# Loading all of k ahead of q and giving the first weight products banks of their own, in a cross-covariance attention and SwiGLU kernel

## The chip, the cores and the metric

The kernel runs on one core of a Trainium2 chip. The metric is the time of one execution on the device in microseconds (us), the median of several; the profile's span of the same execution is about 2 us shorter, because it runs from the first instruction to the last. The engines are called PE (matrix products), PEld (its weight loads), ACT (ScalarE), DVE (VectorE), POOL (GpSimd, which issues the casting loads here) and SP.

## The reference

Four batches of 6016 rows by 256 channels go through attention across channels, and the result through a gated feed-forward block:

```python
qn = q / (norm(q, axis=1) + 1e-6)           # q, k, v: (4, 6016, 256)
kn = k / (norm(k, axis=1) + 1e-6)
s = kn.transpose(0, 2, 1) @ qn / tau        # (4, 256, 256), tau = 1
a = softmax(s, axis=-1)
x = (v @ a).reshape(24064, 256)
g = x @ w_gate                              # (24064, 1536)
out = (silu(g) * (x @ w_val)) @ w_out       # (24064, 256)
```

## The kernel before

The kernel folds the attention matrix into the weights: per batch it forms Wg = a @ w_gate and Wv = a @ w_val, and a main loop then runs v through Wg, Wv and w_out. The work on batch b + 1 (squares, products of k and q, softmax, folding) is spread over the loop of batch b. For batch 0 nothing can hide it, so there is a prologue of some 41 us, and the change is in that prologue and the first steps of the loop only.

PSUM is the memory that PE writes its products to. The kernel lays it out in eight banks and gives each a job: two rotating banks each for the loop's gate and value products (tags "g" and "v"), two rotating ones for outputs (tag "o"), one for the products of k and q ("kq") and one for small sums ("misc"):

```python
psum_gv = tile_pool(name="psum_gv", bufs=2, space=PSUM)   # tags "g" and "v": 4 banks
psum_o  = tile_pool(name="psum_o",  bufs=2, space=PSUM)
psum_kq = tile_pool(name="psum_kq", bufs=1, space=PSUM)
psum_m  = tile_pool(name="psum_m",  bufs=1, space=PSUM)
```

Loads of k and q come in groups of four slabs, k three groups ahead of q. All squares of k are on DVE, those of q (but for the very last pair) on ACT, and PE adds up rows and forms the products as groups arrive:

```python
for g, which in order:                  # k0 k1 k2 k3 q0 k4 q1 ... k11 q8 q9 q10 q11
    if which == 0 and g == NG - 1:
        first_last_q(0, ts)             # the last q group: squares, row copy, products, column sums
        continue
    for t in ts:
        if which == 0:
            gemm1_pair(0, t)
        first_row_sums(0, t, which, first_square(0, t, which, on_dve=(which == 1)), ...)
```

At the end of `first_softmax` the first four folding products ("units" 0 to 3: two of w_gate, two of w_val, 512 columns each) are made in halves, because the loop's first steps need only the lower half. Both halves of a unit share one bank:

```python
for u in range(4):
    wp_evacuate(b, u, units[u], lo)                # ACT for even units, DVE for odd ones
nc.scalar.preload_act_table(ACT.Silu)
for u in range(4):
    for jh in range(CH):
        wp_matmul(b, u, jh, units[u], hi)          # the upper half of the same bank
    wp_evacuate(b, u, units[u], hi, on_dve=True)
```

The loop's step then makes one gate and one value product, a SiLU on ACT and a product on DVE, and in the first chunk two further units after each step:

```python
def gv_step(b, ci, f, sv):
    ...                                            # g_ps and v_ps, two matmuls of 512 columns each
    nc.scalar.activation(silu, g_ps, ACT.Silu)
    nc.vector.tensor_mul(sv[:, f, :], silu, v_ps)

for f in range(FH):                                # 12 steps
    gv_step(b, ci, f, sv)
    if gi == 0:
        for u in range(4 + 2 * f, min(6 + 2 * f, 12)):
            wp_unit(0, u, psum_o, "o")
```

Of the kernel before, what the change touches and what calls it, by code (L numbers as in the profile page):

```python
# [17 lines left out]
def kernel(  # L18
# [11 lines left out]
    nc = tc.nc  # L30
# [145 lines left out]
            nc.tensor.matmul(state[b, "ss", which], ones_bf, sq[:, s, :],  # L176
                             start=(t == 0 and s == 0), stop=(t == t_last and s == pm - 1))

    def first_last_q(b, ts):

        sqs = [first_square(b, t, 0, on_dve=(t == NP - 1)) for t in ts]
        row = work.tile([1, C], FP32, tag="row")
        nc.vector.tensor_copy(row, state[b, "ss", 0][0:1, :])
        for t in ts:
            gemm1_pair(b, t)
        cols = psum_gv.tile([P, CH], FP32, tag="g")
        for h in range(CH):
            nc.tensor.matmul(cols[:, h:h + 1], row[0:1, h * P:(h + 1) * P],
                             ones_f[0:1, 0:1], start=(h == 0), stop=False,
                             skip_group_check=True)  # L190
        for t, sq in zip(ts, sqs):
            pm = pairs[t][1]
            for s in range(pm):
                for h in range(CH):
                    nc.tensor.matmul(cols[:, h:h + 1], sq[:, s, h * P:(h + 1) * P],
                                     ones_bf[:, 0:1], start=False,
                                     stop=(t == ts[-1] and s == pm - 1),
                                     skip_group_check=True)
        state[b, "cols"] = cols

    def first_root(dst, src):
        nc.scalar.activation(dst, src, ACT.Ln)
# [5 lines left out]
        nc.vector.tensor_scalar_add(ink, in0=ink, scalar1=1e-6)  # L208
        state[b, "ink"] = ink

    def first_inv_k(b, h):
        part = state[b, "ink"][:, h * P:(h + 1) * P]
        nc.vector.reciprocal(part, part)

    def first_softmax(b):
        kq, ink = state[b, "kq"], state[b, "ink"]
        inq = work.tile([P, CH], FP32, tag="inq")
        first_root(inq, state[b, "cols"])
        s_f = work.tile([P, CH, C], FP32, tag="s_f")
        nc.vector.tensor_mul(s_f[:, 0, :], kq[:, 0, :], ink)  # L220
        nc.vector.tensor_scalar_add(inq, in0=inq, scalar1=1e-6)
        nc.vector.reciprocal(inq, inq)
        if inv_tau != 1.0:
            nc.vector.tensor_scalar_mul(inq, in0=inq, scalar1=inv_tau)
        nc.vector.tensor_mul(s_f[:, 1, :], kq[:, 1, :], ink)
        transpose_first_v()
        keep_warm(3)
        for h in range(CH):
            evacuate_first_v(h)
        exT = attn.tile([P, CH, C], BF16, tag="exT")  # L230
        state[b, "exT"] = exT
        rs = psum_m.tile([P, CH], FP32, tag="misc")
        for jh in range(CH):
            nc.scalar.activation(exT[:, jh, :], s_f[:, jh, :], ACT.Exp,
                                 scale=inq[:, jh:jh + 1])


        units = []
        for u in range(2 * CH):
            unit_ps = psum_gv.tile([P, WP], FP32, tag="gv"[u % 2])  # L240
            units.append(unit_ps)

        def row_sum(jh):
            for ih in range(CH):
                nc.tensor.matmul(rs[:, ih:ih + 1], exT[:, jh, ih * P:(ih + 1) * P],
                                 ones_bf[:, 0:1], start=(jh == 0 and ih == 0),
                                 stop=(jh == CH - 1), skip_group_check=True)

        HW = WP // 2
        lo, hi = slice(0, HW), slice(HW, WP)  # L250
        row_sum(0)
        wp_matmul(b, 0, 0, units[0], lo)
        wp_matmul(b, 1, 0, units[1], lo)
        row_sum(1)
        finish_rs(b, rs)
        wp_matmul(b, 0, 1, units[0], lo)
        wp_matmul(b, 1, 1, units[1], lo)
        for u in (2, 3):
            for jh in range(CH):
                wp_matmul(b, u, jh, units[u], lo)  # L260
        for u in range(4):
            wp_evacuate(b, u, units[u], lo)
        nc.scalar.preload_act_table(ACT.Silu)
        for u in range(4):
            for jh in range(CH):
                wp_matmul(b, u, jh, units[u], hi)
            wp_evacuate(b, u, units[u], hi, on_dve=True)

    def norm_acc(b, t):
        q_sb, k_sb = qk_tiles[b]  # L270
# [96 lines left out]

    wp_units = [(wc, w, ih) for wc in range(NWC) for w in range(2) for ih in range(CH)]

    def wp_matmul(b, u, jh, ps, part=slice(0, WP)):  # L370
        wc, w, ih = wp_units[u]
        cols = slice(wc * WP + part.start, wc * WP + part.stop)
        nc.tensor.matmul(ps[:, part], state[b, "exT"][:, jh, ih * P:(ih + 1) * P],  # L373
                         (w_gate_sb, w_val_sb)[w][:, jh, cols],
                         start=(jh == 0), stop=(jh == CH - 1), skip_group_check=True)

    def wp_evacuate(b, u, ps, part=slice(0, WP), on_dve=False):
        wc, w, ih = wp_units[u]
        scale = state[b, "smr"][:, ih:ih + 1]
        cols = slice(wc * WP + part.start, wc * WP + part.stop)  # L380
        dst = state[b, "W"][w][:, ih, cols]
        if u % 2 == 0 and not on_dve:
            nc.scalar.activation(dst, ps[:, part], ACT.Copy, scale=scale)
        else:
            nc.vector.tensor_scalar_mul(dst, in0=ps[:, part], scalar1=scale)

    def wp_unit(b, u, pool=psum_m, tag="misc"):

        ps = pool.tile([P, WP], FP32, tag=tag)
        for jh in range(CH):  # L390
            wp_matmul(b, u, jh, ps)
        wp_evacuate(b, u, ps)

    def gv_step(b, ci, f, sv):
        cs, cm = chunks[ci]
# [87 lines left out]


    NG = len(groups)
    K_AHEAD = 3
    order = []
    for g in range(NG + K_AHEAD):
        if g < NG:
            order.append((g, 1))  # L490
        if g >= K_AHEAD:
            order.append((g - K_AHEAD, 0))
    for n, (g, which) in enumerate(order):
        load_qk(0, g, which)
        if n == 8:
# [6 lines left out]
    load_w(1)  # L502
    load_w(2)
    nc.gpsimd.dma_start(out=w_out_sb, in_=moe_w_out.rearrange("(h l) d -> l h d", l=P))
    keep_warm(10)
    T_COLS = groups[NG - 1][0] // 2
    for g, which in order:
        gs, gm = groups[g]
        ts = range(gs // 2, (gs + gm + 1) // 2)
        if which == 0 and g == NG - 1:  # L510
            first_last_q(0, ts)
            continue
        for t in ts:
            if which == 0:
                gemm1_pair(0, t)
            first_row_sums(0, t, which, first_square(0, t, which, on_dve=(which == 1)),
                           (T_COLS if which == 0 else NP) - 1)
        if which == 0:

            after_k = g - (NG - 1 - K_AHEAD)  # L520
            if after_k == 0:
                first_norm_k(0)
                nc.vector.tensor_copy(ident, identf)
            elif 1 <= after_k <= CH:
                first_inv_k(0, after_k - 1)
    first_softmax(0)
    NFIRST = 2 * CH

    prev = None
    for gi, (b, ci) in enumerate(allc):  # L530
        sv = svpool.tile([P, FH, CS * P], BF16, tag="sv")
        for f in range(FH):
            gv_step(b, ci, f, sv)
            if gi == 0:
                for u in range(NFIRST + 2 * f, min(NFIRST + 2 * f + 2, len(wp_units))):
                    wp_unit(0, u, psum_o, "o")
            if prev is not None:
                prev.emit(prev.cm)
            if b + 1 < B:
# [40 lines left out]
```

## Time and profile before

| | |
|---|---|
| time, median of 3 runs | 823.39 us (823.39 to 823.43) |
| span of the profiled run | 821.8 us (that run took 823.9 us) |
| PE busy after 41.07 us | 769.53 of 780.73 us |
| start of the loop's first product | 41.07 us |

This is the start of the loop's third step in the timeline of PE (columns: start, duration, engine, line, operation, output and inputs, shape, count):

```profile
44.52 0.59 PE L404 MATMUL g_ps<-vT_new,Wg 128*128 128x512 bf16 x2
```

By then the kernel before has made units 4 to 7; the changed kernel only 4 and 5.

### The profile page before, as it was taken

The page shows a single profiled execution, that of the slowest core. Times are in us where ns is not written, and L with a number is a line of the kernel's source. Part 1 is how long each engine was busy: PE and PEld are TensorE (multiplying, and loading weights), DVE is VectorE, ACT ScalarE, POOL GpSimd, SP SyncE. Part 2 cuts the span into 40 slices and gives each one's busy share as a digit, 9 for nine tenths or more (in the row PEclk, how much of TensorE's full clock was granted, in tenths as well). Part 3 has the DMA queues.
Part 4 walks back from the last instruction along what each step waited for, and adds up shares of the span by engine and source line. Part 5 has one row for each costly group of instructions (what it writes and reads, how often), then busy time and mean ns, then how long its engine had stood idle before and what let it go on. Part 6 is the DMA issues. An engine that isn't in the chain of part 4 may idle for free.

```text
span 821.8 us, 13520 instructions
## 1 busy us (share of the span) xinstructions
PE 800.2 (97%) x4937; PEld 489.6 (60%) x5024; DVE 552.4 (67%) x870; ACT 461.8 (56%) x826; POOL 90.1 (11%) x171
## 2 busy tenths in 40 slices
PE   7799999999999999999999999999999999999998
PEld 4556566665665566565565656666556565666656
DVE  5576888675655888867556688877665555555554
ACT  2566777555445677645545677755544544544543
POOL 5433000133200000024300000013000000000000
PEclk9999999999999999999999999999999999999999
DMA  9999912169942121129991111125912112112101
GB/s 88 145 160 134 135 39 65 39 119 140 144 90 46 39 65 45 47 52 147 143 150 52 46 52 39 40 65 107 166 39 65 45 40 65 52 39 65 49 26 58
DMA packets 92673, 64.57 MB, mean 79 GB/s; under 512 B 52560, under 2 KB 91472, under 8 KB 91856
## 3 DMA queue, kind: packets, MB, share of 16 engines
q0 software_dynamic: 18656, 27.01, 26.0%
q1 hardware_dynamic: 73952, 36.71, 18.4%
q8 instruction: 39, 0.64, 0.3%
q14 instruction: 26, 0.21, 0.1%
HBM read 78.64 MB, written 36.70 MB: 140 GB/s over the span
## 4 chain that ended last, share of the span: by engine, by line
PE 92%; DMA 3%; ACT 2%; DVE 2%; issue 1%; POOL 0%; DVEq 0%; ACTq 0%; POOLq 0%
PE o_new L432 30%; PE v_ps L404 29%; PE g_ps L404 28%; DMA q_sb<-in_q_dram 2%; PE ps L373 2%; PE kq_new L149 2%; ACT sq L274 1%; DVE sv L408 1%; DMA k_sb<-in_k_dram 1%; DVE acc_new L283 1%; PE cs L291 0%; PE ss_new L176 0%; ACT sq L166 0%; ACT silu L407 0%; PE unit_ps L373 0%
## 5 line engine op out<-in xcount | busy, mean ns | idle before, releaser
L408 DVE TENSOR_TENSOR sv<-silu,v_ps 128x512 bf16<-128x512 bf16 (+1 forms) x576 | 382.6, 673 | 220.1 <-ACT silu L407 218.9
L407 ACT ACTIVATE silu<-g_ps 128x512 bf16<-128x512 f32 (+1 forms) x576 | 337.5, 587 | 305.2 <-PE g_ps L404 252.1
L432 PE MATMUL o_new<-w_out_sb,sv 128*128 128x256 bf16 x2256 | 338.4, 273 | 1.5
L404 PE MATMUL v_ps<-vT,Wv 128*128 128x512 bf16 (+1 forms) x1100 | 324.3, 374 | 6.2 <-DVE sv L408 3.5
L404 PE MATMUL g_ps<-vT,Wg 128*128 128x512 bf16 (+1 forms) x1075 | 319.7, 375 | 0.2
L432 PEld LDWEIGHTS <-sv 128*128 128x128 bf16 x2256 | 220.7, 98 | 140.8
L404 PEld LDWEIGHTS <-Wv 128*128 128x128 bf16 x1152 | 112.7, 98 | 135.0 <-issue 5.4
L404 PEld LDWEIGHTS <-Wg 128*128 128x128 bf16 x1152 | 107.1, 98 | 27.6 <-issue 0.2
L283 DVE TENSOR_TENSOR acc_new<-acc_new,sq 128x512 f32<-128x512 f32 x135 | 93.3, 691 | 23.6 <-ACT sq L274 21.2
L274 ACT ACTIVATE sq<-q_sb 128x512 bf16<-128x512 fp8e5 x72 | 44.3, 615 | 0.0
L274 ACT ACTIVATE sq<-k_sb 128x512 bf16<-128x512 fp8e5 x72 | 44.1, 612 | 0.0
L149 PE MATMUL kq_new<-k_sb,q_sb 128*128 128x512 fp8e5 x184 | 43.3, 317 | 0.3 <-DMA k_sb<-in_k_dram 0.3
L295 POOL TENSOR_TENSOR inv<-inv,half 128x4 f32<-128x4 f32 x3 | 3.1, 1035 | 343.9 <-DVE inv L294 343.9
L441 ACT COPY o_sb<-o_new 128x512 f32<-128x512 f32 x48 | 28.1, 585 | 14.0 <-PE o_new L432 13.7
L443 DVE COPY o_sb<-o_new 128x512 f32<-128x512 f32 (+1 forms) x48 | 31.8, 662 | 3.0 <-PE o_new L432 3.0
L104 POOL DMA_DIRECT2D q_sb<-in_q_dram x48 | 26.1, 544 | 40.1 <-DMA q_sb<-in_q_dram 15.1
L104 POOL DMA_DIRECT2D k_sb<-in_k_dram x48 | 25.9, 540 | 39.5 <-DMA q_sb<-in_q_dram 20.8
L112 POOL DMA_DIRECT2D vb<-in_v_dram x47 | 23.6, 505 | 23.3 <-DMA k_sb<-in_k_dram 14.2
L176 PE MATMUL ss_new<-sq,ones_bf 128*128 128x256 bf16 x91 | 18.3, 285 | 7.5 <-DVE sq L163 6.2
L163 DVE TENSOR_TENSOR sq<-k_sb 128x512 bf16<-128x512 fp8e5 (+1 forms) x24 | 15.2, 681 | 14.2 <-DMA k_sb<-in_k_dram 12.5
L166 ACT ACTIVATE sq<-q_sb 128x512 bf16<-128x512 fp8e5 x23 | 13.0, 619 | 20.1 <-DMA q_sb<-in_q_dram 16.6
L149 PEld LDWEIGHTS <-q_sb 128*128 128x256 fp8e5 x184 | 23.1, 140 | 2.0 <-DMA q_sb<-in_q_dram 0.8
(79 smaller groups left out, 164.5 us busy)
## 6 DMA issues: line engine op xcount, KB each, us to landing
out_dram<-o_sb SPq DMA_DIRECT2D x92, 256.0 KB, 2.4
vb<-in_v_dram POOLq DMA_DIRECT2D x43, 256.0 KB, 10.7
k_sb<-in_k_dram POOLq DMA_DIRECT2D x44, 128.0 KB, 11.6
q_sb<-in_q_dram POOLq DMA_DIRECT2D x44, 128.0 KB, 11.8
w_gate_sb<-in_moe_w_gate_dram POOLq DMA_DIRECT2D x3, 256.0 KB, 9.5
w_val_sb<-in_moe_w_val_dram POOLq DMA_DIRECT2D x3, 256.0 KB, 9.6
w_out_sb<-in_moe_w_out_dram POOLq DMA_DIRECT2D x1, 768.0 KB, 14.3
vb<-in_v_dram POOLq DMA_DIRECT2D x4, 192.0 KB, 4.5
```

Of the source, the lines that this page charges most:

```text
L104: nc.gpsimd.dma_start(out=dst[:, gs:gs + gm, :], in_=src[b].rearrange("(p s) c -> p s c", s=NS)[:, gs:gs + gm, :])
L112: nc.gpsimd.dma_start(out=vb[:mv, :].rearrange("(p s) c -> p (s c)", s=cm), in_=v[b, cs * P:cs * P + mv, :].rearrange("(p s) c -> p (s c)" ...
L149: nc.tensor.matmul(kq[:, jh, :], q_sb[:, ps:ps + 2, js], k_sb[:, ps:ps + 2, :], start=(t == 0 and jh == 0), stop=last, perf_mode=DR, skip_ ...
L176: nc.tensor.matmul(state[b, "ss", which], ones_bf, sq[:, s, :], start=(t == 0 and s == 0), stop=(t == t_last and s == pm - 1))
L274: nc.scalar.activation(sq[:, :pm, which, :], qk_tiles[b][which][:, ps:ps + pm, :], ACT.Square)
L283: nc.vector.tensor_add(acc, acc, sq[:, s, :, :])
L404: nc.tensor.matmul(dst[:, :mv], W[:, kk, fs], vT[:, kk, :mv], start=(kk == 0), stop=(kk == CH - 1))
L407: nc.scalar.activation(silu[:, :mv], g_ps[:, :mv], ACT.Silu)
L408: nc.vector.tensor_mul(sv[:, f, :mv], silu[:, :mv], v_ps[:, :mv])
L432: nc.tensor.matmul(self.o_ps[:, j % 2, :], self.sv[:, f, j * P:(j + 1) * P], w_out_sb[:, f, :], start=(f == 0), stop=(f == FH - 1))
L441: nc.scalar.copy(o_sb[:, :m, :], self.o_ps[:, :m, :])
L443: nc.vector.tensor_copy(o_sb[:, :m, :], self.o_ps[:, :m, :])
```

## The change

The intent: load and square all of k first, so that its norm and inverse (now in quarters) are done long before q ends; share the squares of each group between ACT and DVE; take the column sums of the last two q groups directly; and give the upper halves of the first units banks of their own, so that they need not wait until the lower halves are evacuated. The core of the diff:

```diff
-    K_AHEAD = 3
-    order = []
-    for g in range(NG + K_AHEAD):
...
+    order = [(g, 1) for g in range(NG)] + [(g, 0) for g in range(NG)]
...
-    keep_warm(10)
-    T_COLS = groups[NG - 1][0] // 2
+    G_COLS = NG - 2
+    T_COLS = groups[G_COLS][0] // 2
...
+        sqs = [first_square(0, t, which, on_dve=(t % 2 == 1)) for t in ts]
+        if which == 0:
+            if g == G_COLS:
+                first_row_copy(0)
+            for t in ts:
                 gemm1_pair(0, t)
+            if g == G_COLS:
+                first_cols(0)
...
-            unit_ps = psum_gv.tile([P, WP], FP32, tag="gv"[u % 2])
+            unit_ps = psum_gv.tile([P, HW], FP32, tag="gv"[u % 2])
...
-            wp_evacuate(b, u, units[u], lo)
+            wp_evacuate(b, u, units[u], lo, u % 2 == 1)
+        for u in range(2):
+            wp_unit(b, u, psum_o, "o", hi)
         nc.scalar.preload_act_table(ACT.Silu)
-        for u in range(4):
-            for jh in range(CH):
-                wp_matmul(b, u, jh, units[u], hi)
-            wp_evacuate(b, u, units[u], hi, on_dve=True)
...
             gv_step(b, ci, f, sv)
             if gi == 0:
-                for u in range(NFIRST + 2 * f, min(NFIRST + 2 * f + 2, len(wp_units))):
-                    wp_unit(0, u, psum_o, "o")
+                for u in range(2 * f + 2, min(2 * f + 4, len(wp_units))):
+                    if f == 0:
+                        wp_unit(0, u, psum_o, "o", hi, on_dve=True)
+                    else:
+                        wp_unit(0, u, psum_o, "o")
```

More of the change, by code (lines that the diff above doesn't have):

```diff
@@ L177, in first_row_sums, with first_row_copy, first_cols @@
                              start=(t == 0 and s == 0), stop=(t == t_last and s == pm - 1))
-    def first_last_q(b, ts):
-        sqs = [first_square(b, t, 0, on_dve=(t == NP - 1)) for t in ts]
+    def first_row_copy(b):
         row = work.tile([1, C], FP32, tag="row")
         nc.vector.tensor_copy(row, state[b, "ss", 0][0:1, :])
-        for t in ts:
-            gemm1_pair(b, t)
+        state[b, "row"] = row
+    def first_cols(b):
+        row = state[b, "row"]
         cols = psum_gv.tile([P, CH], FP32, tag="g")
@@ L190, in first_last_q, with first_col_sums @@
                              skip_group_check=True)
-        for t, sq in zip(ts, sqs):
-            pm = pairs[t][1]
-            for s in range(pm):
-                for h in range(CH):
-                    nc.tensor.matmul(cols[:, h:h + 1], sq[:, s, h * P:(h + 1) * P],
-                                     ones_bf[:, 0:1], start=False,
-                                     stop=(t == ts[-1] and s == pm - 1),
-                                     skip_group_check=True)
-        state[b, "cols"] = cols
+        state[b, "cols"] = cols
+    def first_col_sums(b, t, sq):
+        cols = state[b, "cols"]
+        pm = pairs[t][1]
+        for s in range(pm):
+            for h in range(CH):
+                nc.tensor.matmul(cols[:, h:h + 1], sq[:, s, h * P:(h + 1) * P],
+                                 ones_bf[:, 0:1], start=False,
+                                 stop=(t == NP - 1 and s == pm - 1),
+                                 skip_group_check=True)
     def first_root(dst, src):
@@ L209, in first_norm_k, with first_inv_k @@
         state[b, "ink"] = ink
-    def first_inv_k(b, h):
-        part = state[b, "ink"][:, h * P:(h + 1) * P]
+    def first_inv_k(b, n):
+        part = state[b, "ink"][:, n * (C // 4):(n + 1) * (C // 4)]
         nc.vector.reciprocal(part, part)
@@ L235, in first_softmax @@
                                  scale=inq[:, jh:jh + 1])
-        units = []
-        for u in range(2 * CH):
-            unit_ps = psum_gv.tile([P, WP], FP32, tag="gv"[u % 2])
-            units.append(unit_ps)
         def row_sum(jh):
@@ L247, in row_sum @@
                                  stop=(jh == CH - 1), skip_group_check=True)
-        HW = WP // 2
-        lo, hi = slice(0, HW), slice(HW, WP)
+        units = []
+        for u in range(2 * CH):
+            unit_ps = psum_gv.tile([P, HW], FP32, tag="gv"[u % 2])
+            units.append(unit_ps)
         row_sum(0)
@@ L368, with wp_matmul, wp_evacuate @@
     wp_units = [(wc, w, ih) for wc in range(NWC) for w in range(2) for ih in range(CH)]
-    def wp_matmul(b, u, jh, ps, part=slice(0, WP)):
+    HW = WP // 2
+    full, lo, hi = slice(0, WP), slice(0, HW), slice(HW, WP)
+    def wp_matmul(b, u, jh, ps, part):
         wc, w, ih = wp_units[u]
         cols = slice(wc * WP + part.start, wc * WP + part.stop)
-        nc.tensor.matmul(ps[:, part], state[b, "exT"][:, jh, ih * P:(ih + 1) * P],
+        nc.tensor.matmul(ps, state[b, "exT"][:, jh, ih * P:(ih + 1) * P],
                          (w_gate_sb, w_val_sb)[w][:, jh, cols],
-                         start=(jh == 0), stop=(jh == CH - 1), skip_group_check=True)
-    def wp_evacuate(b, u, ps, part=slice(0, WP), on_dve=False):
+                         start=(jh == 0), stop=(jh == CH - 1))
+    def wp_evacuate(b, u, ps, part, on_dve):
         wc, w, ih = wp_units[u]
@@ L381, in wp_evacuate, with wp_unit @@
         dst = state[b, "W"][w][:, ih, cols]
-        if u % 2 == 0 and not on_dve:
-            nc.scalar.activation(dst, ps[:, part], ACT.Copy, scale=scale)
-        else:
-            nc.vector.tensor_scalar_mul(dst, in0=ps[:, part], scalar1=scale)
-    def wp_unit(b, u, pool=psum_m, tag="misc"):
-        ps = pool.tile([P, WP], FP32, tag=tag)
+        if on_dve:
+            nc.vector.tensor_scalar_mul(dst, in0=ps, scalar1=scale)
+        else:
+            nc.scalar.activation(dst, ps, ACT.Copy, scale=scale)
+    def wp_unit(b, u, pool=psum_m, tag="misc", part=full, on_dve=None):
+        ps = pool.tile([P, part.stop - part.start], FP32, tag=tag)
         for jh in range(CH):
-            wp_matmul(b, u, jh, ps)
-        wp_evacuate(b, u, ps)
+            wp_matmul(b, u, jh, ps, part)
+        wp_evacuate(b, u, ps, part, u % 2 == 1 if on_dve is None else on_dve)
     def gv_step(b, ci, f, sv):
@@ L485 @@
     NG = len(groups)
-    K_AHEAD = 3
-    order = []
-    for g in range(NG + K_AHEAD):
-        if g < NG:
-            order.append((g, 1))
-        if g >= K_AHEAD:
-            order.append((g - K_AHEAD, 0))
+    order = [(g, 1) for g in range(NG)] + [(g, 0) for g in range(NG)]
     for n, (g, which) in enumerate(order):
@@ L509 @@
         ts = range(gs // 2, (gs + gm + 1) // 2)
-        if which == 0 and g == NG - 1:
-            first_last_q(0, ts)
-            continue
-        for t in ts:
-            if which == 0:
-                gemm1_pair(0, t)
-            first_row_sums(0, t, which, first_square(0, t, which, on_dve=(which == 1)),
-                           (T_COLS if which == 0 else NP) - 1)
+        sqs = [first_square(0, t, which, on_dve=(t % 2 == 1)) for t in ts]
[3 more added lines that the diff above has]
+            for t in ts:
+                gemm1_pair(0, t)
+            if g == G_COLS:
+                first_cols(0)
+        for t, sq in zip(ts, sqs):
+            if which == 0 and g >= G_COLS:
+                first_col_sums(0, t, sq)
+            else:
+                first_row_sums(0, t, which, sq, (T_COLS if which == 0 else NP) - 1)
         if which == 0:
-            after_k = g - (NG - 1 - K_AHEAD)
-            if after_k == 0:
+            if g == 0:
                 first_norm_k(0)
                 nc.vector.tensor_copy(ident, identf)
-            elif 1 <= after_k <= CH:
-                first_inv_k(0, after_k - 1)
+            elif g <= 4:
+                first_inv_k(0, g - 1)
     first_softmax(0)
-    NFIRST = 2 * CH
     prev = None
@@ L534 @@
             if gi == 0:
-                for u in range(NFIRST + 2 * f, min(NFIRST + 2 * f + 2, len(wp_units))):
-                    wp_unit(0, u, psum_o, "o")
+                for u in range(2 * f + 2, min(2 * f + 4, len(wp_units))):
+                    if f == 0:
+                        wp_unit(0, u, psum_o, "o", hi, on_dve=True)
+                    else:
+                        wp_unit(0, u, psum_o, "o")
             if prev is not None:
```

## The prediction

> **What bounds the kernel now.** I read the page first, then one table of busy time by stretch, then the timeline of each engine between 30 and 45 us.
>
> ```profile
> span 821.8 us, 13520 instructions
> PE 800.2 (97%) x4937; PEld 489.6 (60%) x5024; DVE 552.4 (67%) x870; ACT 461.8 (56%) x826; POOL 90.1 (11%) x171
> ```
>
> The table of busy time splits the span at the first product of the main loop (41.07 us); its columns are length, busy time of PE, PEld, DVE, ACT and POOL, granted clock, DMA share and GB/s:
>
> ```profile
> 0.00:41.07 41.07, 30.71 (x190) 19.16 (x192) 22.30 (x45) 17.73 (x33) 21.61 (x44) 0.96 1.06 117
> 41.07:821.80 780.73, 769.53 (x4749) 470.40 (x4833) 530.08 (x826) 444.12 (x794) 68.54 (x127) 1.00 0.42 77
> ```
>
> After 41.07 us PE is busy 769.53 of 780.73 us: it sets the pace, and the change touches none of that work except the first steps of the loop. So the whole question is how many tenths of a microsecond sooner or later PE gets to the end of the first weight products. The prologue can't shrink far either, because it waits for loads:
>
> ```profile
> 24.77 0.53 POOL L104 DMA_DIRECT2D q_sb<-in_q_dram  x1 [0.73 <-DMA k_sb<-in_k_dram]
> ...
> 34.00 0.71 POOL L477 DMA_DIRECT2D w_gate_sb<-in_moe_w_gate_dram  x1 [0.60 <-DMA q_sb<-in_q_dram]
> 34.94 0.70 POOL L477 DMA_DIRECT2D w_val_sb<-in_moe_w_val_dram  x1 [0.23 <-DMA q_sb<-in_q_dram]
> 36.16 1.05 POOL L504 DMA_DIRECT2D w_out_sb<-in_moe_w_out_dram  x1 [0.52 <-DMA v_sb<-in_v_dram]
> 37.44 0.52 POOL L112 DMA_DIRECT2D vb<-in_v_dram  x1 [0.23 <-DMA w_gate_sb<-in_moe_w_gate_dram]
> 38.76 0.57 POOL L104 DMA_DIRECT2D q_sb<-in_q_dram  x1 [0.80 <-DMA w_val_sb<-in_moe_w_val_dram]
> ```
>
> Each issue on POOL waits for the load eight places before it, so it dates that load's landing. PE's own wait for an earlier q load ended 0.25 us before the POOL issue that waited for the same load (31.20 against 31.45), so I take 0.25 off: the last q group but one lands at about 33.75, the last (issued in the first line, 24.77) at 34.7, the first v at 35.9, the first gate weights at 37.2, the first value weights at 38.5. Before that, loads follow each other every 1.25 us.
>
> The path from the last q to the main loop, from the timelines of PE, DVE and ACT:
>
> ```profile
> 35.68 0.41 DVE L183 COPY row<-ss_new 1x256 f32<-1x256 f32 x1
> ...
> 36.15 0.60 PE L188 MATMUL cols<-ones_f,row 1*128 1x1 f32 x4
> ...
> 36.68 0.30 PE L195 MATMUL cols<-ones_bf,sq 128*128 128x1 bf16 x6
> ...
> 37.02 0.17 ACT L202 ACTIVATE inq<-cols 128x2 f32<-128x2 f32 x1 [1.29 <-PE cols L195]
> ...
> 37.86 0.91 ACT L234 ACTIVATE exT<-s_f,inq 128x256 bf16<-128x256 f32 x2 [0.44 <-DVE inq L222]
> ...
> 40.04 0.60 PE L373 MATMUL unit_ps<-w_gate_sb,exT 128*128 128x256 bf16 x4 [0.34 <-ACT Wg L383]
> ...
> 40.37 1.28 ACT L263 ACT_TABLE_LOAD   x1
> ...
> 41.70 0.60 ACT L407 ACTIVATE silu<-g_ps 128x512 bf16<-128x512 f32 x1
> ...
> 42.32 0.69 DVE L408 TENSOR_TENSOR sv<-silu,v_ps 128x512 bf16<-128x512 bf16 x1
> ```
>
> The last q lands at 34.7, but ACT works off five squares of q until 35.73 and the row of sums is copied only after that. The line at 40.04 is the wait for the half-filled bank that the change aims at. The last two lines matter most below: the first SiLU and the first product on DVE come only after the table load.
>
> **What the Trainium skill says.** "PSUM — Partial Sum Buffer", section "PSUM bank collisions raise a hardware error": two engines must not be on the same bank and partitions at once, and the guard is by bank, not by address. The trace agrees: matmuls into the upper half of a bank wait for the evacuation of its lower half (40.04, 0.34 us). "ScalarE: Activation LUTs", section "What ACT_TABLE_LOAD costs", gives about 1283 ns for the load and a drain of 1380 ns besides; the trace has the 1.28 us, and SiLU starts 0.05 us after it ends, so I count no drain behind it. "TensorE: Matmul & The Clock Gate", section "Part 1: The HAM clock gate": the array runs at half rate until it has been busy for about 3.4 us, and ACT and DVE take their instructions strictly in order. Both show: ten 512-wide warm-up products start 0.43 us apart against 0.22 us later, and the granted clock is 0.50 from 12 to 14 us; DVE runs in program order throughout.
>
> **The change part by part.**
>
> 1. Load order. The same 24 loads of the same bytes at 1.25 us each: nothing after them lands earlier or later. Cost 0.
>
> 2. Squares split over ACT and DVE. ACT 0.61 and DVE 0.69 us for a pair, one each per 1.25 us load, so both keep up; the backlog of ACT at the end (34.7 to 35.73) disappears. In a q group PE has 4 products of 0.11 and 4 row sums of about 0.11 to 0.15 us, 0.9 to 1.0 us: it keeps up at full clock.
>
> 3. Column sums for the last two q groups. Group 10 lands at 33.75: its DVE square ends at 34.45, the row copy (0.41) at 34.85, the turn into columns starts on PE at 34.9 and takes 0.52 to the next weight load, 8 column sums 0.2 (to 35.65). Then the 4 products of the last group (0.4) and its 6 sums (0.3): columns at about 36.3, against 37.02 in the trace. **Gain 0.7 us**, of which I allow only 0.5 to 0.7, because PE does it in order and an extra wait there costs 0.2. The quarters of the inverse (1.75 us in all) lie far ahead of it, as before.
>
> 4. The chain behind shifts with it: exponentials at 37.15, sums, first gate products at 37.75, the value products at 38.5 (their weights land just then, so that bounds the gain), all four lower halves done at 38.95. The scale is ready near 38.75; the four lower evacuations end at about 39.65 (0.47 each, 0.37 to 0.40 apart on each engine).
>
> 5. Banks of their own. Units 0 and 1 upper follow at once (0.44, to 39.4) without the wait of 0.34 to 0.5 us. The first loop step's products then start at about 39.4 to 39.6 instead of 41.07, but with the four upper matmuls of units 2 and 3 still to do. **Gain so far about 1.1 us.**
>
> 6. The price. ACT now evacuates the upper half of unit 0 ahead of the table load: 39.6 to 40.0, table load to 41.3, SiLU 41.35 to 41.95, the DVE product 41.97 to 42.66. In the changed kernel's order on DVE this product stands **before** the two upper evacuations of units 2 and 3. These therefore run from about 42.65 to 43.1 and to 43.5. The upper halves share two rotating banks with the next units, and PE's first matmul of unit 4 has a wait on DVE in the changed order, which the old order has not. PE comes to it at about 41.4 and must stand until 43.15: a **new wait of about 1.7 us**. With units 4 and 5 (0.86) PE is at the third loop step at 44.0; with the 0.5 us gain in step 3, everything 0.25 later, at 44.3.
>
> The old kernel does the third step at 44.52 with two more units (6 and 7, 4 x 0.216 = 0.86 us) done, so the like point is 43.66. **Sum: 44.0 to 44.3 minus 43.66 = 0.35 to 0.65 us slower.** After that the units run one loop step later, and I find no more waits: ACT and DVE each have 0.60 + 0.69 and 0.69 + 0.75 us per 1.73 us of PE. Nothing later gives it back, since PE is 98.6% busy.
>
> 7. Ten warm-up products removed: they run from 1.72 to 5.5 us, before the first k square at 5.29 is done; no cost at the start.
>
> **The rivals.** A, the intended gain: if the wait in step 6 is short (the SiLU early, or buffers freed sooner than I read), PE keeps most of the 1.1 us: about 822.2. For it: the wait at 40.04 and the ACT backlog are real. Against: the table load is on ACT before anything can release DVE. I give it 15%. B, cold clock: without the warm-up and with only four row sums per load, the array is at half rate when q begins. A q group then costs 8 x 0.21 = 1.7 us against 1.25 of load, a backlog of up to 2 us, worked off at 0.3 us a group. In the trace a busy array came back to full clock within 3.7 us (11.25 to 14.98), so twelve groups suffice. If it drops again near the new wait of 1.7 us, 3.4 us at half rate cost some 1.7 us: about 825.5. I give it 10%. C, the gain hidden by the weights: value weights at 38.5 leave 0.6 us for everything before them, which is in the sum already.
>
> **Range and chances.** 823.39 plus 0.5 is 823.9. A pulls the low end to 822.7, B the high end to 825.1. 2% is 16.5 us, more than a third of the whole prologue; only a load order that falls apart could do that.
>
> **What would show it.** Right: inq's logarithm on ACT near 36.3 to 36.6; no wait of the upper products on ACT; table load ending at 41.3 to 41.6; a PE wait of 1.3 to 1.8 us before the first product of unit 4, released by a DVE evacuation into Wv; then the like point about 0.5 us late, and the rest of the span unchanged at 780 us. Wrong: that wait under 0.5 us and the time near 822 (step 6 failed); or columns still at 37 (step 3 failed); or a clock below 1.00 after 30 us (B).

## The result

The changed kernel took **823.95 us** (median of 5 runs, 823.84 to 824.05) against 823.41 us (823.39 to 823.59) for the kernel before: half a microsecond slower, ratio 1.0006 with an interval of 0.9992 to 1.0021. Ratios here are the mean time of one kernel's runs over that of the other's of the same rounds, so not quite the ratio of the medians quoted.

The table of busy time of the changed kernel, with the same split and columns as in the prediction (length, busy time of PE, PEld, DVE, ACT and POOL, granted clock, DMA share, GB/s):

```profile
0.00:41.07 41.07, 30.25 (x191) 19.07 (x192) 22.63 (x45) 20.64 (x35) 21.94 (x45) 1.00 1.06 116
41.07:821.90 780.83, 773.21 (x4829) 469.67 (x4826) 529.82 (x825) 443.77 (x794) 68.50 (x127) 1.00 0.42 77
```

Against the lines of before nothing large has moved: the stretch after 41.07 us is 780.83 us long against 780.73. The difference is within a few microseconds around 41 us, and only the timeline of the changed kernel shows it, from the landing of the first v to the third loop step:

```profile
35.76 1.05 POOL L499 DMA_DIRECT2D w_out_sb<-in_moe_w_out_dram  x1 [0.53 <-DMA v_sb<-in_v_dram]
...
36.07 0.17 ACT L205 ACTIVATE inq<-cols 128x2 f32<-128x2 f32 x1 [1.09 <-PE cols L199]
...
37.01 0.91 ACT L237 ACTIVATE exT<-s_f,inq 128x256 bf16<-128x256 f32 x2 [0.54 <-DVE inq L225]
...
39.89 1.28 ACT L265 ACT_TABLE_LOAD   x1
...
41.18 1.09 ACT L408 ACTIVATE silu<-g_ps 128x512 bf16<-128x512 f32 x2
41.81 0.69 DVE L409 TENSOR_TENSOR sv<-silu,v_ps 128x512 bf16<-128x512 bf16 x1 [1.87 <-ACT silu L408]
...
42.42 0.87 DVE L384 TENSOR_SCALAR Wv<-ps,smr 128x256 bf16<-128x256 f32 x2
42.95 1.02 PE L374 MATMUL ps<-w_gate_sb,exT 128*128 128x512 bf16 x4 [1.42 <-DVE Wv L384]
...
43.81 0.59 PE L405 MATMUL g_ps<-vT_new,Wg 128*128 128x512 bf16 x2
```

Read it from the end. At 42.95 PE starts unit 4, after standing 1.42 us for an evacuation into Wv on DVE (L384). The two evacuations into Wv run from 42.42 only, because DVE has the first loop product (41.81) ahead of them; that product waits for the first SiLU (41.18), and this for the table load on ACT (39.89 to 41.17). The third step starts at 43.81; the like point of before is 43.66. That is 0.15 us, not 0.5, and this is where the two traces must be laid side by side with care: the first line says that the first v had landed by 35.76 us here, in the trace of before only by 36.16. Loads differ by that much from run to run, as the repeat of the kernel before will show.

Where the gain went is visible as well. The logarithm of the column sums starts 0.31 us after the first line here (36.07) and 0.86 us after it in before (37.02 after 36.16). The wait on the half-filled bank at 40.04 in before has no counterpart. The gain is real, and the wait at 42.95 takes more than all of it.

### The profile page after: what moved, and what is told of

The parts are those of the page before. It is cut to its first block, busy times and chain, and to the rows that moved or that the text cites. A ratio compares the mean times of both kernels' runs of the same rounds, so it can differ in the third digit from the quotient of the medians.

```text
span 821.9 us, 13597 instructions
## 1 busy us (share of the span) xinstructions
PE 803.5 (98%) x5018; PEld 488.7 (59%) x5018; DVE 552.4 (67%) x870; ACT 464.4 (57%) x828; POOL 90.4 (11%) x171
## 4 chain that ended last, share of the span: by engine, by line
PE 92%; DMA 3%; ACT 2%; DVE 2%; issue 1%; POOL 0%; DVEq 0%; ACTq 0%; POOLq 0%
PE o_new L433 29%; PE v_ps L405 29%; PE g_ps L405 29%; DMA q_sb<-in_q_dram 2%; PE ps L374 2%; PE kq_new L149 2%; DMA k_sb<-in_k_dram 1%; ACT sq L272 1%; DVE sv L409 1%; DVE acc_new L281 1%; POOL k_sb L104 0%; ACT silu L408 0%; PE cs L289 0%; PE ps L308 0%; ACT L265 0%
## 5 line engine op out<-in xcount | busy, mean ns | idle before, releaser
L405 PE MATMUL v_ps<-vT,Wv 128*128 128x512 bf16 (+1 forms) x1128 | 330.3, 374 | 3.0 <-DVE sv L409 3.0
L405 PE MATMUL g_ps<-vT,Wg 128*128 128x512 bf16 (+1 forms) x1128 | 331.1, 375 | 0.0
L281 DVE TENSOR_TENSOR acc_new<-acc_new,sq 128x512 f32<-128x512 f32 x135 | 93.3, 691 | 23.4 <-ACT sq L272 20.8
L272 ACT ACTIVATE sq<-q_sb 128x512 bf16<-128x512 fp8e5 x72 | 44.2, 615 | 0.0
L149 PE MATMUL kq_new<-k_sb,q_sb 128*128 128x512 fp8e5 x184 | 39.7, 308 | 0.6 <-DMA q_sb<-in_q_dram 0.6
L176 PEld LDWEIGHTS <-ones_bf 128*128 128x128 bf16 x87 | 10.1, 118 | 16.1 <-issue 11.6
L374 PE MATMUL ps<-w_gate_sb,exT 128*128 128x512 bf16 (+1 forms) x48 | 13.4, 370 | 1.4 <-DVE Wv L384 1.4
```

The lines of the kernel that those rows point to most:

```text
L149: nc.tensor.matmul(kq[:, jh, :], q_sb[:, ps:ps + 2, js], k_sb[:, ps:ps + 2, :], start=(t == 0 and jh == 0), stop=last, perf_mode=DR, skip_ ...
L176: nc.tensor.matmul(state[b, "ss", which], ones_bf, sq[:, s, :], start=(t == 0 and s == 0), stop=(t == t_last and s == pm - 1))
L272: nc.scalar.activation(sq[:, :pm, which, :], qk_tiles[b][which][:, ps:ps + pm, :], ACT.Square)
L281: nc.vector.tensor_add(acc, acc, sq[:, s, :, :])
L374: nc.tensor.matmul(ps, state[b, "exT"][:, jh, ih * P:(ih + 1) * P], (w_gate_sb, w_val_sb)[w][:, jh, cols], start=(jh == 0), stop=(jh == CH ...
L405: nc.tensor.matmul(dst[:, :mv], W[:, kk, fs], vT[:, kk, :mv], start=(kk == 0), stop=(kk == CH - 1))
```

## The experiments

Twelve kernels ran, in three lots of four, five rounds each. All gave correct results, and the record counts every run as in the fast state. At its threshold of 2% every verdict, that of the change included, is "same", so tenths of a microsecond are read here from traces and from how far the single runs lie apart. In the lots the kernel before had medians of 823.35, 823.48 and 823.38 us (9, 11 and 9 runs).

My theory: the front of the prologue gains about half a microsecond; the new banks lose about one, because the two rotating output banks are held by the upper halves of units 2 and 3 until DVE, in its order, has done a product that hangs on ACT's table load. The rivals: the difference is noise; the loads bound everything; PE waits for data rather than for a bank; the cold clock costs.

### Both kernels again

No edit.

> The kernel before, once more, for the noise of time and trace. If the 0.5 us between the two kernels is real: 823.4 us within 0.1, ratio to before 1.000 within 0.0003. The first trace of before had a span of 821.8 us in a run of 823.9 us, half a microsecond above its timed runs, so this trace should have a span nearer 821.3 and its first loop step sooner than 41.07 us (about 40.6). Rival (the two kernels differ only by noise): runs of this one spread as far as 823.9 too.

> The changed kernel, once more. If the difference is real: 823.9 us, ratio 1.0006 within 0.0002, and again PE stands about 1.4 us before the first matmul of unit 4, released by the DVE evacuation into Wv. Rival (noise): ratio within 0.0002 of 1.

Measured: before 823.50 us (823.22 to 823.87), ratio 1.0001; changed 823.98 us (823.69 to 824.67), ratio 1.0009. The difference of half a microsecond is there again, though a single run of either kernel can reach the other's range. The new trace of before, in its timeline:

```profile
35.55 1.05 POOL L504 DMA_DIRECT2D w_out_sb<-in_moe_w_out_dram  x1 [0.51 <-DMA v_sb<-in_v_dram]
...
37.25 0.91 ACT L234 ACTIVATE exT<-s_f,inq 128x256 bf16<-128x256 f32 x2 [0.43 <-DVE inq L222]
...
43.91 0.59 PE L404 MATMUL g_ps<-vT_new,Wg 128*128 128x512 bf16 x2
```

The span is 821.1 us, and every point lies 0.6 us earlier than in the first trace: the first v landed by 35.55 instead of 36.16, the third step starts at 43.91 instead of 44.52. The whole prologue hangs on the landing of the loads and moves with it. So traces are compared from here on with the first line, the POOL issue that waits for the first v, as zero:

| kernel | that issue | logarithm | exponential | like point | like point after the issue | span less like point |
|---|---|---|---|---|---|---|
| before | 36.16 | 37.02 | 37.86 | 43.66 | 7.50 | 778.1 |
| before again | 35.55 | 36.41 | 37.25 | 43.05 | 7.50 | 778.1 |
| changed | 35.76 | 36.07 | 37.01 | 43.81 | 8.05 | 778.1 |
| changed again | 35.44 | 35.71 | 36.69 | 43.48 | 8.04 | 778.1 |
| front only | 35.56 | 35.87 | 36.81 | 42.61 | 7.05 | 778.1 |
| banks only | 35.64 | 36.51 | 37.35 | 44.15 | 8.51 | 778.2 |

(The like point is the start of the third step, less 0.86 us where two more units have been made.) The last column is the same for all: what comes after the third step does not change, so the like point decides the time. The column before it gives the change as 0.55 us, in both pairs of traces.

### The order on DVE

The two upper evacuations of units 2 and 3 are emitted between the SiLU and the product of the first step:

```diff
-        nc.vector.tensor_mul(sv[:, f, :mv], silu[:, :mv], v_ps[:, :mv])
+        if between is not None:
+            between()                    # step 0 of chunk 0: units 2 and 3, upper halves
+        nc.vector.tensor_mul(sv[:, f, :mv], silu[:, :mv], v_ps[:, :mv])
```

> The changed kernel with one thing moved: on DVE the two upper evacuations of units 2 and 3 come before the first product of silu and v_ps instead of after it; PE and ACT keep their order. My theory (the in-order DVE passes the table load on to PE's banks): the 1.42 us wait before unit 4 goes to under 0.1, the third loop step starts near 42.3 instead of 43.8, and the time is 1.4 us lower, 822.5 us, ratio to before 0.9989. Rival (another resource, the SiLU or the landing of weights, would end the wait soon after anyway): a wait of over 0.7 us stays at g_ps or v_ps and the time drops by less than 0.7 us.

Measured: 822.66 us (822.59 to 822.92), ratio 0.9992; 1.3 us below the changed kernel. PE's timeline, from unit 4 on:

```profile
41.33 1.03 PE L374 MATMUL ps<-w_gate_sb,exT 128*128 128x512 bf16 x4
...
42.20 0.59 PE L405 MATMUL g_ps<-vT_new,Wg 128*128 128x512 bf16 x2
...
43.06 1.31 PE L374 MATMUL ps<-w_val_sb,exT 128*128 128x512 bf16 x4
```

Unit 4 follows without a wait, the third step starts at 42.20 as expected. The third line shows what is left: four matmuls that take 0.86 us elsewhere are spread over 1.15 (the next step starts at 44.21), because unit 7 waits for the bank of unit 5, whose evacuation DVE does only after two loop products. The rival falls: no other wait of any size takes the place of the one removed. With this one change of order the kernel is faster than before, by 0.7 us, though the interval of the ratio, 0.9978 to 1.0006, still holds 1.

### The front alone

Load order, squares, column sums and quarters of the change; units, banks and loop steps of the kernel before. The edit is the change less these hunks:

```diff
-            unit_ps = psum_gv.tile([P, HW], FP32, tag="gv"[u % 2])
+            unit_ps = psum_gv.tile([P, WP], FP32, tag="gv"[u % 2])
...
-        for u in range(2):
-            wp_unit(b, u, psum_o, "o", hi)
         nc.scalar.preload_act_table(ACT.Silu)
+        for u in range(4):
+            for jh in range(CH):
+                wp_matmul(b, u, jh, units[u], hi)
+            wp_evacuate(b, u, units[u], hi, on_dve=True)
```

> The change without its banks: load order, squares, column sums and quarters as changed, the first weight products and the loop's first steps as before. My theory (the front gains, the banks lose): everything after the columns 0.85 us sooner than before, 822.6 us, ratio 0.9990. Rival (the front gains nothing because loads bound it, and the sooner columns in the changed trace are only loads that happened to land 0.4 us sooner in that run): 823.0 to 823.4 us.

Measured: 823.20 us (822.99 to 823.39), ratio 0.9997. By the time alone this is the rival's range, and my 0.85 us was wrong: I had read it from two traces whose loads landed 0.40 us apart. The rival's reason is wrong too. Its trace can be laid on that of before again, where the loads landed within 0.01 us:

```profile
36.81 0.91 ACT L237 ACTIVATE exT<-s_f,inq 128x256 bf16<-128x256 f32 x2 [0.54 <-DVE inq L225]
...
43.47 0.59 PE L407 MATMUL g_ps<-vT_new,Wg 128*128 128x512 bf16 x2
```

The exponential is at 36.81 against 37.25, the third step at 43.47 against 43.91, the span 820.7 against 821.1. The front gains 0.44 us at equal landing. The medians show 0.15, with a scatter of 0.4 to 0.5 us within each kernel; the trace is the better witness. The median span is 820.8 us here and 821.2 in the nine runs of before, 0.4 us less, as in the traces. Here 2.29 to 2.49 us of the time lie outside the span, in before 2.06 to 2.25; why, no run shows. The front's parts (load order, squares, column sums) were not run one by one, so the 0.44 us belong to all of them together.

### The banks alone

The other hunks on the kernel before: half-width units in banks of their own, units 2 and 3 upper in the first loop step, one step later for the rest. In short:

```diff
-            unit_ps = psum_gv.tile([P, WP], FP32, tag="gv"[u % 2])
+            unit_ps = psum_gv.tile([P, HW], FP32, tag="gv"[u % 2])
...
+        for u in range(2):
+            wp_unit(b, u, psum_o, "o", hi)
         nc.scalar.preload_act_table(ACT.Silu)
-        for u in range(4):
-            for jh in range(CH):
-                wp_matmul(b, u, jh, units[u], hi)
-            wp_evacuate(b, u, units[u], hi, on_dve=True)
...
+                    if f == 0:
+                        wp_unit(0, u, psum_o, "o", hi, on_dve=True)
```

> The other half alone: load order, squares and column sums as before, the half-width products in banks of their own and the loop's first steps as changed. My theory: the wait on the half-filled bank (0.34 us) goes, but the table load ends near 42.05, the first product on DVE near 43.4, unit 4 starts near 43.85 after a wait of about 1.4 us, and the third loop step is 1.05 us late: 824.45 us, ratio 1.0013. Rival (the banks are harmless and the front is what costs): 823.0 us or less.

Measured: 824.39 us (824.05 to 824.49), ratio 1.0010. The two lines of its timeline that answer to those of the changed kernel:

```profile
40.23 1.28 ACT L262 ACT_TABLE_LOAD   x1
...
43.29 1.02 PE L371 MATMUL ps<-w_gate_sb,exT 128*128 128x512 bf16 x4 [1.41 <-DVE Wv L381]
```

The wait is 1.41 us, as in the changed kernel, and for the same evacuation. In the table above the banks cost 8.51 - 7.50 = 1.01 us and the front brings 7.50 - 7.05 = 0.45; the difference, 0.56, is what the whole change costs (0.55). The two halves add.

### Idle banks for units 4 and 5

```diff
                     if f == 0:
                         wp_unit(0, u, psum_o, "o", hi, on_dve=True)
+                    elif f == 1:
+                        wp_unit(0, u, *((psum_m, "misc"), (psum_kq, "kq"))[u % 2])
                     else:
                         wp_unit(0, u, psum_o, "o")
```

> The changed kernel with units 4 and 5 in the two banks that stand idle then (the one of the small sums and the one of the logits) instead of the two that units 2 and 3 hold. DVE keeps its order. Theory (PE waits for a bank, not for data): the wait before unit 4 goes; what is left is a wait of about 0.7 us at the third step's v_ps for the upper half of Wv (data this time); 0.9 us less than the changed kernel, 823.05 us, ratio 0.9996. Rival (PE waits for the data of Wv, not for a bank): no change, 823.95.

Measured: 822.97 us (822.86 to 823.20), ratio 0.9994, as expected within 0.1 us. Two lines of its timeline:

```profile
41.19 1.03 PE L374 MATMUL ps<-w_gate_sb,exT 128*128 128x512 bf16 x4
...
42.77 0.10 PEld L405 LDWEIGHTS <-Wv 128*128 128x128 bf16 x1 [0.61 <-DVE Wv L384]
```

Unit 4 starts without a wait although DVE's order is that of the change: PE had waited for a bank. What PE then waits for is the second line, a weight load of the third step that stands 0.61 us for the upper half of Wv, this time the data itself.

### The warm-up products back

```diff
+    keep_warm(10)
     G_COLS = NG - 2
```

> The changed kernel with the ten warm-up products back at the start. Theory (the path waits for loads, and the clock has recovered by 20 us in the changed trace): no change, 823.95 us within 0.15. Rival (half rate in the k stage costs time later): 0.5 us or more faster.

Measured: 824.02 us (823.72 to 824.11 in five runs; a sixth took 830.41 us at a mean clock of 0.990, which is why the ratio of means is 1.0018). No change, so the removed products cost nothing. The clock is a story of its own. Row sums of the changed kernel, in PE's timeline:

```profile
12.31 1.01 PE L176 MATMUL ss_new<-sq,ones_bf 128*128 128x256 bf16 x4 [0.22 <-ACT sq L166]
...
20.79 0.61 PE L176 MATMUL ss_new<-sq,ones_bf 128*128 128x256 bf16 x4
```

Four row sums take 1.01 us from their first start to their last end in the k stage and 0.61 in the q stage: 0.21 us apart, then 0.11. The array ran at half rate until about 20 us. Yet the table of busy time (PE busy, granted clock, DMA share, GB/s) gives a clock of 1.00 there:

```profile
12.00:13.00 1.00, 0.78 (x5) 1.00 1.11 103
```

With the warm-up products the same stage is shown at 0.50. So it seems, though no run proves it, that the column knows only changes of the clock and takes 1.00 before the first one. In the trace of before it also reads 1.00 while the warm-up products start 0.43 us apart.

### Two more table loads

```diff
         nc.scalar.preload_act_table(ACT.Silu)
+        nc.scalar.preload_act_table_set("natural_log_exp_and_others")
+        nc.scalar.preload_act_table(ACT.Silu)
```

> The changed kernel with the suspected cost enlarged: two more table loads (back to the old set and again to SiLU's) behind the one that is there, 2 x 1.28 = 2.57 us more on ACT ahead of the first SiLU. Theory (table load, SiLU, DVE product, evacuation and unit 4 are one chain with no slack): PE's wait before unit 4 grows from 1.42 to about 4.0 us and the time by 2.6 us, to 826.5, ratio 1.0038. Rival (the wait is set by something else): less than 1 us more.

Measured: 828.22 us (828.20 to 828.84), ratio 1.0060: 4.27 us above the changed kernel (823.95), where 2.57 were expected. PE's wait is just what was expected, 1.42 + 2.57:

```profile
45.42 1.40 PE L376 MATMUL ps<-w_gate_sb,exT 128*128 128x512 bf16 x4 [3.99 <-DVE Wv L386]
```

The rest is in the table of busy time after it (length, PE busy, granted clock, DMA share, GB/s):

```profile
46.00:47.00 1.00, 1.00 (x4) 0.50 1.33 182
...
49.00:50.00 1.00, 1.00 (x5) 0.82 0.41 58
```

The clock is at 0.50 from just before 46 us until 49.4 us: half a microsecond after PE resumed at 45.42, having stood 4 us, the array fell to half rate. From the start of unit 4 to the fourth step, PE takes 4.28 us here (45.42 to 49.70) and 2.59 in the changed kernel (42.95 to 45.54): 1.69 us for the clock, and 2.57 + 1.69 = 4.26 is the whole. The chain from the table load to unit 4 has no slack, and my number missed because it left out this fall of the clock, which followed the wait of 3.99 us and not that of 1.42. How long a wait brings it on was not measured.

### One more table load

```diff
         nc.scalar.preload_act_table(ACT.Silu)
+        nc.scalar.preload_act_table(ACT.Silu)
```

> The changed kernel with one more load of SiLU's table behind the one that is there: 1.28 us more ahead of the first SiLU. The run with two more loads cost 4.2 us instead of 2.6, and its trace shows the granted clock at 0.50 for some 3.4 us after a wait of 4 us. Theory (one for one, and the rest of the two-load run was the clock): PE's wait before unit 4 is 2.7 us, the clock stays at 1.00, the time is 1.3 us above the changed kernel, 825.25 us, ratio 1.0022. Rival (more than one for one for another reason): 2 us or more.

Measured: 824.02 us (823.99 to 824.18), ratio 1.0007. This experiment failed: the second request for the same table never became an instruction. The trace has one table load there, and as many instructions in all (13597) as that of the changed kernel. It is a third run of the changed kernel, with a wait of 1.41 us, and tells nothing about the question; the run with two loads has to do.

### The table load sooner

```diff
-            wp_unit(b, u, psum_o, "o", hi)
+            wp_unit(b, u, psum_o, "o", hi, on_dve=True)
```

> The changed kernel with the upper half of unit 0 evacuated on DVE instead of ACT, so that the table load has one evacuation less ahead of it (0.37 us). Theory: the table load, the first SiLU, the DVE product and unit 4 come 0.37 us sooner, PE waits about 1.05 us, the time is 823.6 us, ratio 1.0002. Rival (DVE is the bound of this chain, and one more evacuation on it delays): 0.3 us or more slower than the changed kernel.

Measured: 823.66 us (median; 823.45 to 823.86 in four runs, 825.38 in a fifth), ratio 1.0006 because of that fifth. The table load starts at 39.47 instead of 39.89, PE waits 0.95 us:

```profile
42.53 1.02 PE L374 MATMUL ps<-w_gate_sb,exT 128*128 128x512 bf16 x4 [0.95 <-DVE Wv L384]
```

The like point is 7.68 us after the landing instead of 8.05: 0.37 us, as expected. With the two added loads this shows the chain from both sides: what ACT does ahead of the first SiLU reaches PE in full.

### The output weights issued later

```diff
-    nc.gpsimd.dma_start(out=w_out_sb, in_=moe_w_out.rearrange("(h l) d -> l h d", l=P))
...
                 load_v(*allc[gi + VT_AHEAD])
+                if gi == 0:
+                    nc.gpsimd.dma_start(out=w_out_sb, in_=moe_w_out.rearrange("(h l) d -> l h d", l=P))
```

> The changed kernel with the load of the output weights issued one place later, after a load of v whose issue takes half as long. In five traces the reciprocal on DVE ahead of the exponentials starts just when POOL ends that 1.05 us issue. Theory (DVE is held up by the issue on POOL): from inq's second step on ACT to the reciprocal's start 0.44 us again as in the kernel before, not 0.54; 0.1 us sooner behind it, 823.85 us, too little for the times to show, so the trace decides. Rival (chance, or the product just ahead of it on DVE): still 0.54 us.

Measured: 823.71 us (823.48 to 823.90), ratio 1.0003. The reciprocal and the addition ahead of it on DVE, in the changed kernel, then here:

```profile
36.51 0.27 DVE L224 TENSOR_SCALAR inq<-inq 128x2 f32<-128x2 f32 x1
36.81 0.17 DVE L225 RECIPROCAL inq<-inq 128x2 f32<-128x2 f32 x1
```

```profile
36.07 0.17 DVE L224 TENSOR_SCALAR inq<-inq 128x2 f32<-128x2 f32 x1
36.28 0.17 DVE L225 RECIPROCAL inq<-inq 128x2 f32<-128x2 f32 x1
```

In the changed kernel POOL's issue of the output weights ends at 35.76 + 1.05 = 36.81 us, where the reciprocal starts, 0.54 us after the second step on ACT (36.27). Here the reciprocal starts 0.44 us after that step (35.84), as in the kernel before. The exponential comes 1.13 us after the landing of the first v instead of 1.25. It is not the reciprocal that was held up: it takes 0.17 us in both. The addition ahead of it starts 0.24 us after the step on ACT there and 0.23 here, but takes 0.27 us there, until just before the issue ends, and 0.17 here. The other traces agree: the addition takes 0.26 to 0.30 us in all nine in which it starts during that issue, and 0.17 in the five in which it does not. It is not any issue on POOL, though: in three of these five (before, its repeat, banks only) the addition starts 0.02 to 0.03 us into the next issue, that of a v, and is not held up. So the issue of the output weights held DVE up by 0.1 us. The Trainium skill, "SBUF — State Buffer", section "SBUF: two separate sides", says that DVE, in some kinds of operation, and GpSimd contend for a shared port pair: whichever starts first holds it for its whole instruction, and the other is blocked. The section's boxed example is DVE holding back a load's issue. The delay here fits the other order, but no line of the profile names its cause, nor shows that this addition is of such a kind, so the port remains the likely cause, not the shown one.

### All that helped

The order on DVE, the idle banks and the later issue together; the three diffs above, of which the second now reads:

```diff
                 for u in range(2 * f + 2, min(2 * f + 4, len(wp_units))):
-                    wp_unit(0, u, psum_o, "o")
+                    if f == 1:
+                        wp_unit(0, u, *((psum_m, "misc"), (psum_kq, "kq"))[u % 2])
+                    else:
+                        wp_unit(0, u, psum_o, "o")
```

> All that helped in one kernel: the upper evacuations before the first product on DVE, units 4 and 5 in the two idle banks, and the output weights issued one place later. Theory (the gains add): 1.42 us from the order, 0.29 us that the order alone still waits at the second of units 6 and 7, 0.1 us from the issue: 1.8 us below the changed kernel, 822.2 us, ratio to before 0.9985. Rival (one wait hides another): no better than the order alone, 822.65 us.

Measured: **822.18 us** (822.04 to 822.30), ratio to before 0.9984 (0.9971 to 0.9996). The gains add. PE's timeline:

```profile
41.21 1.03 PE L374 MATMUL ps<-w_gate_sb,exT 128*128 128x512 bf16 x4
...
42.08 0.59 PE L405 MATMUL g_ps<-vT_new,Wg 128*128 128x512 bf16 x2
...
42.94 1.03 PE L374 MATMUL ps<-w_val_sb,exT 128*128 128x512 bf16 x4
```

Unit 4, third step, units 6 and 7 follow each other with no wait. It is 1.2 us faster than the kernel before and 1.8 us faster than the changed one, and every run of it is below every run of either.

## Why the prediction was right

It forecast 823.9 us, 0.5 us slower, and the cause; 823.95 us was measured, and the wait is the one named. By its steps:

1. **Load order**: right. With the landing of the first v as zero, nothing shifts. But the dates that the prediction took from the first trace (33.75, 34.7, 38.5) belong to a run in which loads came 0.6 us later than in the repeat. This did no harm to the sum because both sides of it were dated from the same trace, but two of its signs missed by it: the logarithm was forecast at 36.3 to 36.6 and came at 36.07, the end of the table load at 41.3 to 41.6 and came at 41.17. With the 0.40 us by which the first v landed sooner (35.76 against 36.16) both lie inside, at 36.47 and 41.57.
2. **Squares**: right; both engines keep up.
3. **Column sums**: the mechanism right, the term mis-sized. It allowed 0.5 to 0.7 us. The logarithm comes 0.55 us sooner, but the exponential only 0.45, since DVE is held up for 0.1 us by the issue on POOL; the later issue gave that back. The 0.7 was also generous: it sets the end of the columns (36.3) against the start of the logarithm (37.02), and its own terms add up to 36.35 for columns that end at 36.98 in the trace (36.68 + 0.30), 0.63 us. That the column sums brought this gain, rather than the shared squares, is not shown, as the front was run only as a whole.
4. **The chain behind**: right, but the value weights did not bound it, because the gain was smaller. By the prediction's own dating they landed at 38.12 (38.37 less 0.25), and the value products started at 38.25, so only 0.13 us was left.
5. **Banks**: right, the wait at 40.04 is gone.
6. **The price**: right in kind, with PE's wait at unit 4 released by the DVE evacuation into Wv. It measured 1.42 us instead of 1.7. Here the sum slipped: from a first step at 39.4 to 39.6, two steps (0.86 each) and the upper matmuls of units 2 and 3 (0.44) bring PE to unit 4 at 41.6 to 41.8, not 41.4. That PE came there later left the rest as it was, because DVE decides when unit 4 starts. Table load, SiLU and DVE product ran within 0.2 us of the times forecast, but partly by luck: the loads landed 0.40 us sooner, so at equal landing they were 0.2 to 0.3 us late. That is the "0.25 later" which the prediction gives for a gain of only 0.5 us in step 3, and the gain was 0.45. The order on DVE, the idle banks, the longer and the shorter way to the first SiLU each moved it as this step says.
7. **Warm-up products**: right, no gain from putting them back.

The sum of 0.35 to 0.65 us slower came out at 0.55 at equal landing. Of the rivals, A (the intended gain) fails by the wait that stayed, though the order on DVE delivers what A expected. B was right about the half rate in the k stage and wrong about its cost; its fear of a drop at the new wait came true only when that wait was 4 us. C fell.

## What to carry to other kernels

When a tile is moved to a rotating bank to save a wait, ask who releases that bank, and what stands ahead of that release in its engine's order: here an evacuation was ready, but its in-order engine sat behind a product that hung on a table load elsewhere. Here a change of order in the program gained 1.3 us, and other banks 1.0. And lay two traces on the same event, such as the landing of a load, before reading tenths of a microsecond off them: here two runs of one kernel differed by as much as the two kernels.

## What the Trainium skill lacked or had wrong

- "ScalarE: Activation LUTs", section "What ACT_TABLE_LOAD costs": the load is 1.28 us as stated. The drain of 1380 ns is not seen as a cost: in the changed kernel the load started 0.02 us after ACT's last evacuation ended (39.39 + 0.48), and with two more loads three in a row started 1.29 us apart (39.79, 41.08, 42.37) and the SiLU started 0.01 us after the last one ended.
- "TensorE: Matmul & The Clock Gate", section "Part 1: The HAM clock gate": how busy the array must be to leave half rate is not said. In the k stage of the changed kernel it ran four row sums 0.21 us apart in every 1.25 us (about two thirds of the time) from 6 to 18.6 us and stayed at half rate; from then on it ran without a gap, and by 20.8 us it was at full rate. A wait of 1.42 us left the clock at 1.00; after one of 3.99 us it was 0.50 for 3.4 us, and that length agrees with the page.
- The same section warns in general that the clock events of a trace cannot be fully trusted; it does not name this case: the clock read 1.00 for some 14 us before the first change that the trace shows, with row sums 0.21 us apart instead of 0.11.
- "SBUF — State Buffer", section "SBUF: two separate sides": the box tells of a load's issue held back by DVE; what such an issue costs DVE is not sized. Here an addition of two elements per partition on DVE took 0.26 to 0.30 us instead of 0.17 when it started during an issue of 1.05 us on POOL; that the port is the cause is not shown.
